# Recurrent-memory attention: last K projection in two banks, second scores earlier, batched Q/K with streaming weights

## The chip, the cores and the metric

The kernel runs on one core of a Trainium2 chip. The metric is the time of one execution on the device, in microseconds (us). A figure for a kernel is the median of several executions.

## The reference

Two residual blocks. The first is attention in segments with a carried memory; the second is a gated mixing block. The change concerns the first alone.

```
for s in range(64):                                  # 2048 rows in segments of 32
    h = concat(mem, xs)                              # 8 memory rows + 32 rows, 512 wide
    q, k, v = h @ Wq, h @ Wk, h @ Wv                 # 32 heads of 128
    p = softmax(mask(q k^T * scale))                 # 40 x 40 for each head
    o = (p v) @ Wo
    mem = o[:8]                                      # memory of the next segment
    outs.append(o[8:])
```

The memory makes the 64 segments strictly sequential: the first rows of the output of segment s are an input of segment s+1. Q, K and V of the 32 rows of a segment itself do not depend on it. Behind the loop stand a layer norm, a GELU projection, a product with a 2048 x 2048 matrix and an output projection.

## The kernel before, in words

`fast_path` records all instructions of five engines in the order of the program; each engine runs its own in that order, and waits are made from tokens that each instruction reads and writes. On every engine the order of the work is therefore the order in which the Python code calls the helpers. One consequence matters here: an instruction that waits holds back all that is recorded behind it on its engine.

The four projection weights stay in SBUF (`arena`, 4 MB each). The 40 rows of a step are split. The 8 memory rows and the first 24 rows of the segment are in `hT` (transposed, 32 columns a step). The last 8 rows of each segment do not depend on the memory and are projected for 16 segments at once: a chunk (`CK` = 16) has 128 such rows, in `hTe`. Their Q and K go to `QTx` (two buffers, one for each of two chunks), their V over DRAM to `Vx`.

**TensorE in four column tiles.** Most matmuls of the loop use the array as four tiles of 128 rows and 32 columns: the 32 columns of `hT` are the weights of each tile, and the projection matrix streams past, 512 columns at a time; tile c computes another quarter of the output. `tile_mm` (L493) emits such a matmul; with `held` it emits one without a weight load (L496 instead of L495), where the tile still holds the same weights.

**One step of the loop** (L945 on), halves b = 0, 1 of 16 heads each:

- `QK` (L501) computes Q or K of one half into a PSUM bank (`QKB`: banks 0, 1, 6, 7), in four groups over the contraction (dc = 0 to 3). dc 0 and 1 need the memory columns from `mem_out(s-1, 0)`, dc 2 and 3 those from `mem_out(s-1, 1)`, which stands between.
- `QK_evac` (L512) brings them from PSUM to `Tst` (ScalarE, L519), pairing heads so that two bf16 values make one 32-bit word, and VectorE transposes the words into `QT` or `KT` (L532). The last K (half 1) is evacuated in two parts, both after its four groups.
- `qx_copy` (L534, GpSimd) puts the 8 batched query rows beside them for the next step.
- `mask_put` (L544) writes the mask into the scores' banks; `S_half` (L546) adds the scores on top: L554 for 32 keys, L560 for the 8 batched keys (from `QTx`).
- Softmax of a half: `sm_exp` (L568, ScalarE), `sm_sums` (two rounds of matmuls with ones, L575 and L496), `sm_ln` (L586), `sm_rcp` (L590, the reciprocal by Exp of the negative logarithm), `sm_norm` (L594 and L598; half 0 on GpSimd, half 1 on VectorE).
- `V_half` (L600) computes V in four groups, `V_evac` (L615, VectorE) copies it.
- `PV_half` (L617): L623 for 32 keys, L629 for the batched 8, with the array as four row tiles.
- `cT_evac` (L642 ScalarE, L644 VectorE), then `WoX_mm` (L707, output product of the batched rows of an earlier block of 128), then `Wo` in two column halves, `part_evac` (L671, L673) and `mem_out` (L680, with its copy L685).

**Filler.** Between the second sums and `PV_half` stands one group per step that nothing in the step waits for: from the list `gx` a batched V group (`vx_group`, L433; steps 1 to 7, 14, 15) or a batched Q/K group (`qkx_group`, L414; steps 8 to 13 and 16 to 47), or, from step 48, a group of the second block (`z2_group`, L775). All go to PSUM bank 3 (`XB`); their evacuation is recorded behind the four `cT_evac`. A second list (`gv`, bank 5) pours single V groups, ahead of the filler or behind `WoX_mm`. In steps with s % 4 = 3, 1, 2 bank 3 is used once more near the step's end.

A batched Q/K group before: four heads, for each four matmuls of the full array (128 x 128 weights taken from `w_q` or `w_k`, 128 streaming columns of `hTe`), copied in one go to `QTx` (`qkx_evac`, L423 on ScalarE ahead of the loop, L425 on VectorE in it). 26 such groups stand ahead of the loop.

Of the kernel before, what the change touches and what calls it, by code (L numbers as in the profile page):

```python
# [169 lines left out]
def fast_path(nc, st, keep, A_x, A_mem0, A_Wq, A_Wk, A_Wv, A_Wo, A_seg_len, B_w_in, B_w_sp, B_b_sp, B_w_out, out):  # L170
# [9 lines left out]
    DC = D // 128  # L180
# [23 lines left out]
    def region(off, n):  # L204
        return arena[:, off:off + n]
# [5 lines left out]
    QTx = [region(4 * WSZ + i * QX, QX).rearrange("p (m s h k) -> p m s h k", m=2, s=CK, h=H) for i in range(2)]  # L211
# [269 lines left out]
    QKB = {(0, 0): 0, (0, 1): 1, (1, 0): 6, (1, 1): 7}  # L481
    SBK = (0, 1)
# [29 lines left out]
    def QK_evac(s, b, mi, parts=1):  # L512
        bank = QKB[(b, mi)]
        tb = mi
        n = 8 // parts
        for k in range(parts):
            tok = [("T", tb, 0), ("T", tb, 1)] if parts == 1 else [("T", tb, k)]
            cs = slice(64 * n * k, 64 * n * (k + 1))
            act(lambda e, cs=cs: e.activation(out=Tst[:, tb, cs].rearrange("p (hp i r) -> p hp i r", i=32, r=2),  # L519
                                              in_=ps[:, bank, cs].rearrange("p (hp r i) -> p hp i r", r=2, i=32), func=ACT.Copy),  # L520
                reads=[PB(bank)], writes=tok)
        for k in range(parts):
            tok = [("T", tb, 0), ("T", tb, 1)] if parts == 1 else [("T", tb, k)]
            src = Tst[:, tb, 64 * n * k:64 * n * (k + 1)].bitcast(U32)
            hs = slice(n * k, n * (k + 1))
            if mi == 0:
                dst = QT[:, b, hs, :, :].rearrange("p hp q r -> p (hp q r)").bitcast(U32).rearrange("p (hp q) -> p hp q", hp=n)[:, :, 8:40]
                wr = [("QT", b)]
            else:
                dst = KT[:, b, hs, :, :].rearrange("p hp q r -> p (hp q r)").bitcast(U32)  # L530
                wr = [("KT", b, 0), ("KT", b, 1)] if parts == 1 else [("KT", b, k)]
            dve(lambda e, dst=dst, src=src: e.transpose(out=dst, in_=src), reads=tok, writes=wr)  # L532

    def qx_copy(s):  # L534
        j = s % CK
        buf = (s // CK) % 2
        dst = QT[:].rearrange("p b hp q r -> p (b hp) q r")[:, :, 0:8, :].rearrange("p hp q r -> p hp r q")
        src = QTx[buf][:, 0, j, :, :].rearrange("p (hp r) q -> p hp r q", r=2)
        pool(lambda e: e.tensor_copy(out=dst, in_=src), reads=[("QTx", buf, 0, i) for i in range(8)],  # L539
             writes=[("QTe", 0), ("QTe", 1)])  # L540
# [5 lines left out]
    def S_half(s, b):  # L546
# [4 lines left out]
        for g in range(4):  # L551
            for c in range(4):
                hp, r = 2 * c + g // 2, g % 2
                pe(lambda e, hp=hp, r=r, c=c, g=g: e.matmul(  # L554
                    ps[32 * c:32 * c + 32, bank, g * 40:(g + 1) * 40], lhsT=KT[:, b, hp, :, r], rhs=QT[:, b, hp, :, r],
                    start=False, stop=(g == 3), skip_group_check=True, tile_position=(0, 32 * c)),
                    reads=rd, writes=[PB(bank)])
# [339 lines left out]

    def vx_group(ck, n):
# [12 lines left out]
    for ck, i0 in ((1, 10), (2, 0), (3, 0)):  # L911
# [3 lines left out]
        for i in range(i0, 16):  # L915
            qkx_group(ck, i)
# [28 lines left out]
    for s in range(NSEG):  # L945
# [1162 lines left out]
```

## Time and profile before

| | us |
|---|---|
| median of 3 runs | 855.01 (853.56 to 855.67) |
| the profiled execution: its own time | 853.86 |
| its span in the profile | 851.7 |
| busy: TensorE matmul | 837.0 |
| busy: VectorE | 538.8 |
| busy: ScalarE | 427.1 |
| busy: GpSimd | 159.8 |

The granted TensorE clock is full speed throughout. Row forms in the timeline: start, duration, engine, line, operation, output tile <- input tiles, shape, count of merged instructions, and in brackets the idle time of the engine before them. "128*32" in front of a matmul's shape gives rows and columns of the array that it uses: 128*128 is the full array, 128*32 one of four column tiles, 32*128 one of four row tiles. The duration of a matmul runs from its start to its last result, longer than the distance to the next one.

### The profile page before, as it was taken

What the parts mean: (1) busy time and instruction counts of PE and PEld (TensorE: products, weight loads), DVE (VectorE), ACT (ScalarE), POOL (GpSimd) and SP (SyncE); (2) the same over time, 40 slices, a digit from 0 to 9 for tenths busy, and PEclk for the clock granted to TensorE, in tenths of its full rate; (3) what the DMA queues carried; (4) which work ended last, traced back from release to release, by engine and by line L of the source; (5) the groups of instructions that cost most, each with busy time, mean ns of one, the idle gap of its engine ahead of it and who ended that gap; (6) DMA issues with size and microseconds to landing.
All of it is one profiled execution on the core that took longest, in us unless ns stands there. A gap on an engine that the chain in (4) does not pass through costs nothing.

```text
span 851.7 us, 43893 instructions
## 1 busy us (share of the span) xinstructions
PE 837.0 (98%) x20921; PEld 447.0 (52%) x19133; DVE 538.8 (63%) x1256; ACT 427.1 (50%) x1151; POOL 159.8 (19%) x404
## 2 busy tenths in 40 slices
PE   6999999999999999999999999999999999999997
PEld 5754445555555555556555555555554544444443
DVE  3456677676666666676766666767666676553443
ACT  2455565656555655555655555565656566500000
POOL 5111121122121112121212121211112123200000
PEclk9999999999999999999999999999999999999999
DMA  9972322223212122121323222233322369032001
GB/s 319 379 227 59 75 56 57 54 47 82 57 34 75 34 65 62 26 72 47 64 58 85 55 74 51 81 70 85 91 57 80 96 184 366 2 112 105 33 12 40
DMA packets 105614, 77.21 MB, mean 91 GB/s; under 512 B 63304, under 2 KB 90960, under 8 KB 105424
## 3 DMA queue, kind: packets, MB, share of 16 engines
q1 hardware_dynamic: 105424, 74.35, 30.3%
q8 instruction: 159, 2.61, 1.3%
q14 instruction: 31, 0.25, 0.1%
HBM read 42.38 MB, written 21.59 MB: 75 GB/s over the span
## 4 chain that ended last, share of the span: by engine, by line
PE 95%; DMA 2%; SPq 1%; issue 0%; ACT 0%; DVE 0%; POOL 0%; POOLq 0%
PE f_ps L495 46%; PE f_ps L1183 11%; PE f_ps L496 8%; PE f_ps L414 6%; PE f_ps L707 4%; PE f_ps L1300 3%; PE f_ps L623 3%; PE f_ps L1176 2%; PE f_ps L433 2%; PE f_ps L775 2%; PE f_ps L554 1%; PE f_ps L575 1%; DMA f_arena<-in_A_Wk_dram 1%; PE f_ps L629 1%; PE f_ps L439 1%; PE f_ps L680 1%
## 5 line engine op out<-in xcount | busy, mean ns | idle before, releaser
L495 PE MATMUL f_ps<-f_arena,f_hT 128*32 128x512 bf16 x5120 | 359.5, 380 | 0.3
L495 PEld LDWEIGHTS f_ps<-f_arena,f_hT 128*32 128x32 bf16 x5120 | 117.0, 95 | 153.7 <-issue 63.0
L519 ACT ACTIVATE f_Tst<-f_ps 128x512 bf16<-128x512 f32 (+1 forms) x320 | 150.0, 510 | 77.5 <-PE f_ps L495 77.4
L495 PE MATMUL f_ps<-f_arena,f_cT 128*32 128x256 bf16 x3844 | 127.9, 272 | 0.7 <-ACT f_cT L642 0.5
L495 PEld LDWEIGHTS f_ps<-f_arena,f_cT 128*32 128x32 bf16 x3844 | 94.8, 96 | 27.3 <-ACT f_cT L642 18.2
L615 DVE CAST f_V_sb<-f_ps 128x512 bf16<-128x512 f32 x128 | 88.6, 692 | 25.4 <-PE f_ps L495 25.4
L1183 PE MATMUL f_ps<-f_arena 128*128 128x512 bf16 x448 | 100.9, 379 | 0.6 <-DMA f_arena<-wT_d 0.6
L532 DVE STREAM_TRANSPOSE f_QT<-f_Tst 128x256 uint32<-128x256 uint32 x128 | 57.0, 446 | 68.6 <-ACT f_Tst L519 68.5
L496 PE MATMUL f_ps<-f_arena,f_hT 128*32 128x512 bf16 x1024 | 99.8, 379 | 0.0
L539 POOL COPY f_QT<-f_arena 128x256 bf16<-128x256 bf16 x64 | 30.8, 482 | 313.3 <-PE f_ps L560 313.2
L642 ACT ACTIVATE f_cT<-f_ps 128x320 bf16<-128x320 f32 x128 | 49.0, 435 | 49.1 <-PE f_ps L629 49.1
L644 DVE TENSOR_SCALAR f_cT<-f_ps 128x320 bf16<-128x320 f32 x128 | 56.9, 487 | 25.4 <-PE f_ps L629 25.4
L532 DVE STREAM_TRANSPOSE f_KT<-f_Tst 128x128 uint32<-128x128 uint32 (+1 forms) x192 | 64.5, 349 | 12.9 <-ACT f_Tst L519 12.9
L1183 PEld LDWEIGHTS f_ps<-f_arena 128*128 128x128 bf16 x448 | 43.7, 98 | 53.4 <-DVE f_mv L723 1.0
L673 DVE CAST f_part<-f_ps 128x256 bf16<-128x256 f32 x64 | 27.2, 425 | 67.9 <-PE f_ps L495 67.9
L414 PE MATMUL f_ps<-f_hTe,f_arena 128*128 128x128 bf16 x1024 | 66.9, 223 | 2.2 <-DMA f_arena<-in_A_Wq_dram 1.4
L414 PEld LDWEIGHTS f_ps<-f_hTe,f_arena 128*128 128x128 bf16 x1024 | 59.1, 100 | 7.5 <-ACT f_hTe L395 1.6
L586 ACT ACTIVATE f_R_sb<-f_ps 128x160 f32<-128x160 f32 x128 | 39.1, 305 | 35.9 <-PE f_ps L496 32.7
L1189 DVE TENSOR_TENSOR f_arena<-f_ps,f_arena 128x512 f32<-128x512 f32 x28 | 19.3, 690 | 52.9 <-PE f_ps L1183 52.9
L685 ACT ACTIVATE f_hT<-f_ps 128x16 bf16<-128x16 f32 x126 | 23.3, 185 | 53.4 <-PE f_ps L680 53.0
L671 ACT ACTIVATE f_part<-f_ps 128x256 bf16<-128x256 f32 x64 | 24.6, 385 | 48.4 <-PE f_ps L495 48.4
L544 DVE CAST f_ps<-f_mask 128x224 f32<-128x224 bf16 x128 | 47.1, 368 | 0.0
(118 smaller groups left out, 1094.1 us busy)
## 6 DMA issues: line engine op xcount, KB each, us to landing
wT_d<-f_wst SPq DMA_DIRECT2D x32, 256.0 KB, 2.5
f_arena<-wT_d SPq DMA_DIRECT2D x32, 256.0 KB, 4.8
f_arena<-in_A_Wq_dram SPq DMA_DIRECT2D x4, 1024.0 KB, 8.7
f_arena<-in_A_Wk_dram SPq DMA_DIRECT2D x4, 1024.0 KB, 14.3
f_arena<-in_A_Wv_dram SPq DMA_DIRECT2D x4, 1024.0 KB, 14.5
f_arena<-in_A_Wo_dram SPq DMA_DIRECT2D x8, 512.0 KB, 9.5
f_Vx<-vext_d SPq DMA_DIRECT2D x63, 64.0 KB, 2.9
vext_d<-f_Vs SPq DMA_DIRECT2D x24, 128.0 KB, 2.0
```

The lines of the kernel that those rows point to most:

```text
L414: pe(lambda e, h=h, dc=dc, hh=hh: e.matmul(ps[:, bank, hh * 128:(hh + 1) * 128], lhsT=ws[:, dc, h * DH:(h + 1) * DH], rhs=hTe[:, ck % 3, d ...
L495: return e.matmul(out, lhsT=lhsT, rhs=rhs, start=start, stop=stop, skip_group_check=True, tile_position=(0, 32 * c))
L496: return e.add_instruction(mybir.InstMatmult(name=nc.get_next_instruction_name(), ins=[e.lower_ap(rhs), e.lower_ap(lhsT)], outs=[e.lower_a ...
L519: act(lambda e, cs=cs: e.activation(out=Tst[:, tb, cs].rearrange("p (hp i r) -> p hp i r", i=32, r=2), in_=ps[:, bank, cs].rearrange("p (h ...
L532: dve(lambda e, dst=dst, src=src: e.transpose(out=dst, in_=src), reads=tok, writes=wr)
L544: dve(lambda e: e.tensor_copy(out=ps[:, bank, 0:224], in_=mask[:, :]), reads=["mask"], writes=[PB(bank)])
L586: act(lambda e: e.activation(out=R_sb[:, b, :], in_=ps[:, bank, 224:384], func=ACT.Ln, scale=LNS), reads=[PB(bank)], writes=[("R", b)])
L615: dve(lambda e: e.tensor_copy(out=V_sb[:, b, :], in_=ps[:, bank, :]), reads=[PB(bank)], writes=[("V", b)])
L642: act(lambda e: e.activation(out=dst, in_=src, func=ACT.Copy, scale=UNSC), reads=[PB(PVB[c])], writes=[("cT", c)])
L644: dve(lambda e: e.tensor_scalar(out=dst, in0=src, scalar1=UNSC, scalar2=None, op0=ALU.mult), reads=[PB(PVB[c])], writes=[("cT", c)])
L707: pe(lambda e, h=h, g=g, i=8 * qr + bg: e.matmul(ps[32 * g:32 * g + 32, WXB, :], lhsT=cTx[:, rb % 2, i, :], rhs=w_o[:, h, :], start=(i < 4 ...
L1183: pe(lambda e: e.matmul(ps[:, bank, 0:TB], lhsT=z2[:, sc, fb * 128:(fb + 1) * 128], rhs=wTb[tb % 2][:, :, sc, :], start=(n == 0), stop=(n ...
```

## The change

1. **Last K in two banks.** K of half 1 is computed by `K1` as two halves of 8 heads, 256 columns each, in banks 3 and 7. The groups of the two alternate so that one ends two groups ahead of the other; `K1_copy` and `K1_transpose` bring each on alone.
2. **Order and held weights in the first half of a step.** Q's dc 0, K's dc 0 with the same weights, the second half of `mem_out`, K's dc 1, Q's dc 1 with the same weights.
3. **Second scores moved forward.** `S_half(s, 1)` stands behind three of the four V groups of half 0 rather than all four, and `sm_ln(0)` behind `sm_exp(1)` rather than ahead of it. The second sums stand ahead of V's last group of half 1 rather than behind it.
4. **Batched Q/K groups.** `qkr_group` takes the 32 rows of four segments as weights of the four column tiles and streams 16 heads of `w_q` or `w_k` past them, 512 columns a matmul, like the projections of a step. ScalarE pairs the heads into `Tst` (`pair_copy`), VectorE transposes into `QTx`. 36 of the 38 groups in the loop have the new form; the first two keep the old one, as do the 26 ahead of it.
5. **Layout.** Pairs are made of heads that are four apart, `QTx` holds them interleaved, and `qx_copy` moves 32-bit words.

```diff
-    QTx = [region(4 * WSZ + i * QX, QX).rearrange("p (m s h k) -> p m s h k", m=2, s=CK, h=H) for i in range(2)]
+    QTx = [region(4 * WSZ + i * QX, QX).rearrange("p (m s C g k r) -> p m s C g k r", m=2, s=CK, C=H // 8, g=4, r=2) for i in range(2)]
+    QTxU = [region(4 * WSZ + i * QX, QX).bitcast(U32).rearrange("p (m s hp k) -> p m s hp k", m=2, s=CK, hp=H // 2) for i in range(2)]
...
+    KB = (3, 7)
...
+    def K1(s, k, dc, first, last, held):
+        bank = KB[k]
+        sl = slot(s)
+        for c in range(4):
+            rhs = w_k[:, dc, :].rearrange("p (h c i) -> p c h i", c=4, i=32)[:, c, 16 + 8 * k:24 + 8 * k, :]
+            pe(lambda e, c=c, rhs=rhs: tile_mm(e, ps[32 * c:32 * c + 32, bank, 0:256], hT[:, sl, dc, :], rhs, first, last, c, held),
+               ...)
+
+    def K1_copy(k):
+        act(lambda e: e.activation(out=Tst[:, 1, 256 * k:256 * k + 256].rearrange("p (gi r) -> p gi r", r=2),
+                                   in_=ps[:, KB[k], 0:256].rearrange("p (r gi) -> p gi r", r=2), func=ACT.Copy),
+            reads=[PB(KB[k])], writes=[("T", 1, k)])
+
+    def K1_transpose(k):
+        src = Tst[:, 1, 256 * k:256 * k + 256].bitcast(U32)
+        dst = KT[:, 1, 4 * k:4 * k + 4, :, :].rearrange("p hp q r -> p (hp q r)").bitcast(U32)
+        dve(lambda e: e.transpose(out=dst, in_=src), reads=[("T", 1, k)], writes=[("KT", 1, k)])
+
+    def pair_copy(bank, tb):
+        act(lambda e: e.activation(out=Tst[:, tb, :].rearrange("p (C gi r) -> p C gi r", C=2, r=2),
+                                   in_=ps[:, bank, :].rearrange("p (C r gi) -> p C gi r", C=2, r=2), func=ACT.Copy),
+            reads=[PB(bank)], writes=[("T", tb, 0), ("T", tb, 1)])
...
+    def qkr_group(ck, mi, b, r):
+        ws = (w_q, w_k)[mi]
+
+        def f():
+            for dc in range(DC):
+                for c in range(4):
+                    rhs = ws[:, dc, :].rearrange("p (h c i) -> p c h i", c=4, i=32)[:, c, 16 * b:16 * b + 16, :]
+                    pe(lambda e, dc=dc, c=c, rhs=rhs: tile_mm(e, ps[32 * c:32 * c + 32, XB, :], hTe[:, ck % 3, dc, 32 * r:32 * r + 32], rhs,
+                                                              dc == 0, dc == DC - 1, c),
+                       ...)
+
+            def ev():
+                pair_copy(XB, 0)
+                dst = QTxU[ck % 2][:, mi, 4 * r:4 * r + 4, 8 * b:8 * b + 8, :].rearrange("p s hp k -> p hp s k")
+                dve(lambda e: e.transpose(out=dst, in_=Tst[:, 0, :].bitcast(U32)), ...)
+            return ev
...
-        QK(s, 0, 0, (0, 1), 0, 3)
+        QK(s, 0, 0, (0,), 0, 3)
+        QK(s, 0, 1, (0,), 0, 2, 0)
         if s > 0:
             mem_out(s - 1, 1)
-        QK(s, 0, 1, (1, 0), 1, 2, None if s else 1)
-        QK(s, 0, 0, (2, 3), 0, 3)
+        QK(s, 0, 1, (1,), 0, 2)
+        QK(s, 0, 0, (1, 2, 3), 0, 3, 1)
...
-        for mi in range(2):
-            QK(s, 1, mi, ((2, 0, 1, 3), (3, 0, 1, 2))[mi], (2, 3)[mi], (3, 2)[mi], (2, 3)[mi])
-            QK_evac(s, 1, mi, 1 + mi)
+        QK(s, 1, 0, (2, 0, 1, 3), 2, 3, 2)
+        QK_evac(s, 1, 0)
+        K1(s, 0, 3, True, False, True)
+        K1(s, 1, 3, True, False, True)
+        K1(s, 0, 0, False, False, False)
+        K1(s, 1, 0, False, False, True)
+        K1(s, 0, 1, False, False, False)
+        K1(s, 0, 2, False, True, False)
+        K1_copy(0)
+        K1(s, 1, 2, False, False, True)
+        K1(s, 1, 1, False, True, False)
+        K1_copy(1)
+        for k in range(2):
+            K1_transpose(k)
         S_half(s, 0)
         sm_exp(0)
-        V_half(s, 0, (0,))
-        if s > 0:
+        if s == 0:
+            V_half(s, 0)
+            V_evac(0, "dve")
+            sm_sums(0)
+            S_half(s, 1)
+        else:
+            V_half(s, 0, (0,))
             V_half(s, 1, (0,), 0)
-        V_half(s, 0, (1, 2, 3))
-        V_evac(0, "dve")
-        sm_sums(0)
-        sm_ln(0)
-        S_half(s, 1)
+            V_half(s, 0, (1, 2))
+            sm_sums(0)
+            S_half(s, 1)
+            V_half(s, 0, (3,))
+            V_evac(0, "dve")
         lastop["s"] = sops[s] = em.by_eng["pe"][-1]
         sm_exp(1)
+        sm_ln(0)
         sm_rcp(0)
         if s == 0:
             for n in range(2, 4):
                 start_v(n)
-        V_half(s, 1, (1, 2, 3) if s > 0 else range(DC))
+            V_half(s, 1)
+            sm_sums(1)
+        else:
+            V_half(s, 1, (1, 2))
+            sm_sums(1)
+            V_half(s, 1, (3,))
         lastop["v"] = em.by_eng["pe"][-1]
-        sm_sums(1)
         sm_ln(1)
         sm_rcp(1)
```

More of the change, by code (lines that the diff above doesn't have):

```diff
@@ L510, in QK @@
                    reads=[("hTx", (s // 4) % 3), ("hTm", s, dc // 2), ("W", mi, 2 * b), ("W", mi, 2 * b + 1)], writes=[PB(bank)])
[L512 to L532, printed above, removed]
@@ new lines, in QK_evac @@
+    def QK_evac(s, b, mi):
+        pair_copy(QKB[(b, mi)], mi)
+        if mi == 0:
+            dst = QT[:, b, :, :, :].rearrange("p hp q r -> p (hp q r)").bitcast(U32).rearrange("p (hp q) -> p hp q", hp=8)[:, :, 8:40]
+            wr = [("QT", b)]
+        else:
+            dst = KT[:, b, :, :, :].rearrange("p hp q r -> p (hp q r)").bitcast(U32)
+            wr = [("KT", b, 0), ("KT", b, 1)]
+        dve(lambda e: e.transpose(out=dst, in_=Tst[:, mi, :].bitcast(U32)), reads=[("T", mi, 0), ("T", mi, 1)], writes=wr)
@@ L536, in qx_copy @@
         buf = (s // CK) % 2
-        dst = QT[:].rearrange("p b hp q r -> p (b hp) q r")[:, :, 0:8, :].rearrange("p hp q r -> p hp r q")
-        src = QTx[buf][:, 0, j, :, :].rearrange("p (hp r) q -> p hp r q", r=2)
+        dst = QT[:].rearrange("p b hp q r -> p (b hp q r)").bitcast(U32).rearrange("p (hp q) -> p hp q", q=40)[:, :, 0:8]
+        src = QTxU[buf][:, 0, j, :, :]
         pool(lambda e: e.tensor_copy(out=dst, in_=src), reads=[("QTx", buf, 0, i) for i in range(8)],
@@ L552, in S_half @@
             for c in range(4):
-                hp, r = 2 * c + g // 2, g % 2
+                hp, r = 4 * (c // 2) + g, c % 2
                 pe(lambda e, hp=hp, r=r, c=c, g=g: e.matmul(
@@ L896, in qkx_group @@
         gx.append(f)
+    def qkr_group(ck, mi, b, r):
[6 more added lines that the diff above has]
+                                                              dc == 0, dc == DC - 1, c),
+                       reads=[("hTe", ck % 3), ("W", mi, 2 * b), ("W", mi, 2 * b + 1)], writes=[PB(XB)])
+            def ev():
+                pair_copy(XB, 0)
+                dst = QTxU[ck % 2][:, mi, 4 * r:4 * r + 4, 8 * b:8 * b + 8, :].rearrange("p s hp k -> p hp s k")
+                dve(lambda e: e.transpose(out=dst, in_=Tst[:, 0, :].bitcast(U32)), reads=[("T", 0, 0), ("T", 0, 1)],
+                    writes=[("QTx", ck % 2, mi, 4 * b + r)])
+            return ev
+        f.full = True
+        gx.append(f)
     def vx_group(ck, n):
@@ L914, in fast_path @@
             vx_group(2, 1)
-        for i in range(i0, 16):
-            qkx_group(ck, i)
+        if i0:
+            qkx_group(ck, 10)
+            qkx_group(ck, 11)
+        for mi, b in ((0, 0), (0, 1), (1, 0), (1, 1))[3 if i0 else 0:]:
+            for r in range(4):
+                qkr_group(ck, mi, b, r)
     for ck, n0 in ((2, 2), (3, 0)):
```

13 lines of the change are left out of this document (8 added, 5 removed).

## The prediction

> **What bounds the kernel now.** I read the page first, then the waits of TensorE, then the timeline of single steps of the loop, engine by engine.
>
> ```profile
> PE 95%; DMA 2%; SPq 1%; issue 0%; ACT 0%; DVE 0%; POOL 0%; POOLq 0%
> ...
> L495 PEld LDWEIGHTS f_ps<-f_arena,f_hT 128*32 128x32 bf16 x5120 | 117.0, 95 | 153.7 <-issue 63.0
> ...
> L414 PE MATMUL f_ps<-f_hTe,f_arena 128*128 128x128 bf16 x1024 | 66.9, 223 | 2.2 <-DMA f_arena<-in_A_Wq_dram 1.4
> ```
>
> TensorE sets the time: 95% of the chain that ended last. L414 is the batched Q/K matmul: 64 groups of 16, of which 26 stand ahead of the loop and 38 in it. Since matmuls overlap, their durations hide small waits; I take start-to-start distances from the timeline. Here is TensorE in one step with a batched Q/K group (starts in us, duration, engine, line, count):
>
> ```profile
> 300.44 0.27 PE L554 MATMUL f_ps<-f_QT,f_KT 128*32 128x40 bf16 x16
> ...
> 300.57 0.39 PE L495 MATMUL f_ps<-f_arena,f_hT 128*32 128x512 bf16 x4
> 300.79 0.39 PE L496 MATMUL f_ps<-f_arena,f_hT 128*32 128x512 bf16 x4
> 301.00 0.82 PE L495 MATMUL f_ps<-f_arena,f_hT 128*32 128x512 bf16 x12
> 301.65 0.24 PE L575 MATMUL f_ps<-f_E_sb,f_ones 128*32 128x160 bf16 x4
> ...
> 301.75 0.27 PE L554 MATMUL f_ps<-f_QT,f_KT 128*32 128x40 bf16 x16
> ...
> 301.88 0.83 PE L495 MATMUL f_ps<-f_arena,f_hT 128*32 128x512 bf16 x12
> 302.56 0.25 PE L575 MATMUL f_ps<-f_E_sb,f_ones 128*32 128x160 bf16 x4
> ...
> 302.78 1.07 PE L414 MATMUL f_ps<-f_hTe,f_arena 128*128 128x128 bf16 x16
> 303.78 0.27 PE L623 MATMUL f_ps<-f_E_sb,f_V_sb 32*128 32x40 bf16 x16
> ...
> 303.99 0.28 PE L623 MATMUL f_ps<-f_E_sb,f_V_sb 32*128 32x40 bf16 x16
> ...
> 304.26 0.61 PE L707 MATMUL f_ps<-f_arena,f_cTx 128*32 128x512 bf16 x8
> ...
> 304.92 1.05 PE L495 MATMUL f_ps<-f_arena,f_cT 128*32 128x256 bf16 x32
> 305.79 0.28 PE L496 MATMUL f_ps<-f_arena,f_cT 128*32 128x256 bf16 x4
> ```
>
> I count from the first score matmul of the first half, 300.44 = 0 (S0). Four 512-column matmuls in four column tiles take 0.215 (300.57 to 301.00 is two such groups). So five V groups bring the first sums at 1.21, the second scores (S1) come at 1.31, three more V groups end at 302.53, and the second sums start at 302.56: 0.03 to 0.04 lost. The batched group (L414), then the first PV half at 3.34, the second at 3.55, and the deferred output product (WoX, L707) at 3.82. I sum to WoX, since the work behind it depends on it alone.
>
> The other engines in the same stretch, first ScalarE, then VectorE, then GpSimd:
>
> ```profile
> 300.66 0.66 ACT L519 ACTIVATE f_Tst<-f_ps 128x256 bf16<-128x256 f32 x2 [0.27 <-PE f_ps L495]
> 301.21 0.36 ACT L568 ACTIVATE f_E_sb<-f_ps 128x224 bf16<-128x224 f32 x1
> 301.96 0.31 ACT L586 ACTIVATE f_R_sb<-f_ps 128x160 f32<-128x160 f32 x1 [0.39 <-PE f_ps L496]
> 302.16 0.35 ACT L568 ACTIVATE f_E_sb<-f_ps 128x224 bf16<-128x224 f32 x1
> 302.41 0.33 ACT L590 ACTIVATE f_R_sb<-f_R_sb 128x160 f32<-128x160 f32 x1
> 302.88 0.30 ACT L586 ACTIVATE f_R_sb<-f_ps 128x160 f32<-128x160 f32 x1
> 303.22 0.34 ACT L590 ACTIVATE f_R_sb<-f_R_sb 128x160 f32<-128x160 f32 x1
> ```
>
> ```profile
> 301.08 0.59 DVE L532 STREAM_TRANSPOSE f_KT<-f_Tst 128x128 uint32<-128x128 uint32 x2 [0.20 <-ACT f_Tst L519]
> ...
> 302.75 0.69 DVE L615 CAST f_V_sb<-f_ps 128x512 bf16<-128x512 f32 x1 [0.18 <-PE f_ps L495]
> 303.59 0.34 DVE L594 TENSOR_TENSOR f_E_sb<-f_R_sb,f_E_sb 128x160 bf16<-128x160 f32 x1
> 303.86 0.21 DVE L598 TENSOR_TENSOR f_E_sb<-f_R_sb,f_E_sb 128x64 bf16<-128x64 f32 x1
> ```
>
> ```profile
> 302.88 0.49 POOL L594 TENSOR_TENSOR f_E_sb<-f_R_sb,f_E_sb 128x160 bf16<-128x160 f32 x1 [0.21 <-ACT f_R_sb L590]
> 303.45 0.31 POOL L598 TENSOR_TENSOR f_E_sb<-f_R_sb,f_E_sb 128x64 bf16<-128x64 f32 x1
> ```
>
> The second PV half starts at 303.99, which is 0.06 after VectorE's normalisation ends (303.59 + 0.34 = 303.93). So in such a step TensorE already waits for the softmax there: sums, Ln, Exp, normalise. That is the key to the forecast.
>
> **The change part by part.**
>
> *Batched group.* Sixteen full-array matmuls become four groups of four tiles, 4 x 0.215 = 0.86. Now, second sums to PV is 303.78 - 302.56 = 1.22. A step with the batched V group, whose matmuls already have the new form, shows the other price:
>
> ```profile
> 191.25 0.25 PE L575 MATMUL f_ps<-f_E_sb,f_ones 128*32 128x160 bf16 x4
> ...
> 192.54 0.27 PE L623 MATMUL f_ps<-f_E_sb,f_V_sb 32*128 32x40 bf16 x16
> 192.67 0.21 PE L629 MATMUL f_ps<-f_E_sb,f_Vx 32*128 32x64 bf16 x4
> ...
> 192.95 0.62 PE L707 MATMUL f_ps<-f_arena,f_cTx 128*32 128x512 bf16 x8
> ```
>
> 1.29 there, with five groups of 0.215 in it; four would be 1.08. The group is thus 0.14 cheaper on TensorE: one of two switches of the array's shape goes. 36 steps have it. Whether the 0.14 reaches the end is decided by PV's waits, below.
>
> *Its evacuation* was one VectorE copy; now it is a ScalarE copy of 128x512 and a VectorE transpose, queued behind the context copies. On ScalarE the tightest place is a step with s % 4 = 3, where the WoX copy (L712) follows:
>
> ```profile
> 244.29 0.60 ACT L712 ACTIVATE f_partx<-f_ps 128x512 bf16<-128x512 f32 x1
> 245.31 0.39 ACT L671 ACTIVATE f_part<-f_ps 128x256 bf16<-128x256 f32 x1 [0.42 <-PE f_ps L495]
> ```
>
> The new copy takes the place at 244.29, L712 moves 0.50 back (0.60, less the 0.1 by which such copies overlap, as the 0.66 for two of 0.38 shows) and ends its turn at 245.29; L671, which the next step's memory rows wait for, is due at 245.31. I take nothing. The other end, without overlap, is 0.3 in 9 steps, 2.8 us. In the other steps an idle stretch of ScalarE covers it. VectorE loses a copy of 128x512 (0.69 as in L615) and gains a transpose (two half ones take 0.59): nothing. The 8-row query copy on GpSimd moves half as many elements; it is not waited for.
>
> *Last K in two banks.* Eight groups of 256 columns for four of 512. L495 with 256 columns goes 304.92 to 305.79 for eight groups, 0.87, against 4 x 0.215 = 0.86: +0.01 a step, 63 steps, **+0.6 us**. In return the first ScalarE copy no longer waits for all of K. Now the two copies start at 0.22 and the exp at 0.77; then the first copy starts at 0.00, the second at 0.28 (ScalarE's pace), the exp at 0.55. Transposes: the first from 0.42, the second behind the second copy, 0.66 + 0.03, to 1.01, not 1.23. The K weights can be used 0.06 later (the PV distance above): 1.07.
>
> *S1 moved forward.* Four V groups instead of five before the first sums: 0.99, and S1 at 1.09. Exp 0 ends at 0.91, so 0.97 for the sums. Both are met with 0.02, about the slack of today (301.57 to 301.65, and 301.67 to 301.75, are 0.08 with the 0.06 in them). I take no wait. Fewer loaded and more held weights in the first half of a step cost and bring nothing: a held group (300.79) takes the same 0.215 as a loaded one.
>
> *The softmax behind it.* Exp 1 started 0.41 after S1, held some 0.05 by the Ln ahead of it; now the exp is first: 1.09 + 0.36 = 1.45 to 1.80. The second sums, after V's last group of half 0 and two of half 1, arrive at 1.87: their 0.04 stall goes. But the first Ln is now behind exp 1: 1.70 to 2.01 (one pace of 0.25 as 302.16 to 302.41), its reciprocal exp 2.04 to 2.37. Today that one ends at 2.30. So half 0 has its reciprocals 0.07 *later*, although everything ahead of it is earlier. GpSimd starts 0.14 behind (302.74 to 302.88): 2.51, the second multiply 0.57 on, 3.08 to 3.39. From a step near the end, without filling work, I read how soon TensorE follows GpSimd:
>
> ```profile
> 679.72 0.31 POOL L598 TENSOR_TENSOR f_E_sb<-f_R_sb,f_E_sb 128x64 bf16<-128x64 f32 x1
> ```
>
> ```profile
> 680.08 0.21 PE L629 MATMUL f_ps<-f_E_sb,f_Vx 32*128 32x64 bf16 x4
> ```
>
> 0.05. So the extra-column matmuls of PV half 0 can start at 3.44, and WoX 0.28 later (192.67 to 192.95): **3.72**. Half 1: Ln at about 2.26 (ScalarE is busy until then), reciprocal 2.60 to 2.94; V's evacuation (L615) starts 0.44 after its last group, now at 1.97, so 2.41 to 3.10; normalise 3.03 to 3.10, the second part 0.27 on, plus 0.21: 3.51 to 3.58; WoX follows that by 0.19 (304.07 to 304.26): 3.70 to 3.77. TensorE alone would have PV at 3.15 and WoX near 3.56. So the two softmax chains set it: 3.72 against 3.82, **0.10 a step**, and most of the cheaper group is waited away.
>
> The steps of the last quarter (z2 filler) end in the same chain today, as sums to WoX shows, 1.70 in both:
>
> ```profile
> 567.62 0.25 PE L575 MATMUL f_ps<-f_E_sb,f_ones 128*32 128x160 bf16 x4
> ...
> 569.32 0.62 PE L707 MATMUL f_ps<-f_arena,f_cTx 128*32 128x512 bf16 x8
> ```
>
> So they gain 0.10 too.
>
> **Sum.** 38 steps with a Q/K group and 16 z2 steps: 54 x 0.10 = 5.4. The 9 V steps have one group more ahead of PV and gain only the sums' stall, 9 x 0.04 = 0.4. K in two banks: -0.6. Together **-5.2 us**. The profiled execution took 853.86 (span 851.7), which would become 848.7; the median of the three runs is 855.01, so I name **849.8**.
>
> **Rivals.**
> - *Deeper gain.* GpSimd answers within 0.08 (the distance between its own two, 303.37 to 303.45) now that its query copy ends early, and VectorE starts to normalise at 2.97, right behind the reciprocal: WoX at 3.63, 0.19 a step, 54 x 0.19 - 0.2 = 10 us, **845**. For it: these are lower ends of rows. Against: GpSimd's 0.14 is what this pair shows, and V's evacuation ends at 3.10.
> - *Weights on the path.* If loads of column tiles did not hide, the 13 loaded groups of a step, now 12, would give 117.0 / 1280 = 0.09 (the page's row of loads, 5120 of them): 63 x 0.09 = 5.8 more, **844**. Against it: 300.57, 300.79 and 301.00 are a loaded, a held and a loaded group, equally spaced within 0.01.
> - *No change.* S1 or the sums miss their 0.02 by 0.05 to 0.09 a step, or the ScalarE queue costs its 2.8: **852.4 to 857**.
> - *Slower.* S1 now waits for the last K transpose. If the two transposes don't overlap with the copies as counted but come a whole one (0.31) later, S1 stands at 1.40, and exp, Ln, GpSimd and PV shift with it: 63 x 0.31 = 19.5, so **869**. It decides from 0.08 a step, and 0.13 makes it slower. For it: 0.02 of slack by rows of two decimals. Against: in the same queue today nothing waits.
> - *It doesn't do what it says*: the cheaper group is there but PV waits; that is the forecast itself.
>
> [...]
>
> **How the numbers follow.** Forecast 848 to 852: 0.57. Deeper gain: 0.20. Weights: 0.01. No change: 0.13. Slower: 0.09. A difference of 0.3%, 2.6 us, is about what a measurement here can tell from none. Faster is 0.57 + 0.20 + 0.01 = 0.78. The range 844.5 to 854 holds the forecast, the deeper gain and the lower part of no change, 0.82.
>
> **What would show it.** L414 falls from 1024 to 448 matmuls. Second sums follow the V group ahead without a gap. PV half 0 stops before its L629 for GpSimd by about 0.15 where a Q/K group stands. S1 at 1.09 behind S0. Wrong if S1 stands later than 1.15, if L671 is late where s % 4 = 3, or if WoX comes before 3.65.

## The result, and the profile after

The changed kernel takes 857.4 us (median of 16 executions, 855.75 to 859.3), the kernel before 854.52 (16 executions, 851.92 to 857.1): a ratio of 1.0033, 95% interval 1.0023 to 1.0043. It is 2.9 us slower, where 5.2 us less had been forecast. The profiled execution of after took 858.33 us, with a span of 856.2.

The first place to look is the chain that ended last. This is its line of shares by engine, on the page of after:

```profile
PE 85%; POOL 6%; ACT 4%; issue 2%; DMA 1%; DVE 0%; SPq 0%; POOLq 0%
```

Before, TensorE had 95% of it and GpSimd 0%. Now GpSimd and ScalarE hold 10% of the chain: part of it has moved from TensorE's own work to the softmax that TensorE waits for. The view of the waits of TensorE's weight loads (PEld; what was waited for, us in total, times, longest) is the next place to look. After:

```profile
PEld f_ps L497 <- issue: 71.0, 197, 0.5
...
PEld f_ps L636 <- POOL f_E_sb L607: 25.2, 61, 0.5
...
PEld f_ps L642 <- POOL f_E_sb L611: 9.1, 39, 0.3
```

And the two rows of before that answer to them:

```profile
PEld f_ps L623 <- POOL f_E_sb L594: 5.9, 16, 0.4
...
PEld f_ps L623 <- POOL f_E_sb L598: 3.8, 9, 0.4
```

PV half 0 is L636 and, for the extra columns, L642. By the view, the loads of L636 wait for GpSimd's first multiply (L607) in 61 steps, those of L642 for the second (L611) in 39. But the filler's matmuls run while these loads wait (in the step below they start at 304.60 and take 1.04, and GpSimd's first multiply ends at 305.42), so the timeline has to tell which of the two waits holds the matmuls up. Here is a step with a batched Q/K group, from the timeline of after, TensorE first:

```profile
302.39 0.27 PE L567 MATMUL f_ps<-f_QT,f_KT 128*32 128x40 bf16 x16
...
303.39 0.24 PE L588 MATMUL f_ps<-f_E_sb,f_ones 128*32 128x160 bf16 x4
...
303.49 0.27 PE L567 MATMUL f_ps<-f_QT,f_KT 128*32 128x40 bf16 x16
...
304.28 0.25 PE L588 MATMUL f_ps<-f_E_sb,f_ones 128*32 128x160 bf16 x4
...
304.60 1.04 PE L497 MATMUL f_ps<-f_arena,f_hTe 128*32 128x512 bf16 x16
305.57 0.27 PE L636 MATMUL f_ps<-f_E_sb,f_V_sb 32*128 32x40 bf16 x16
305.97 0.21 PE L642 MATMUL f_ps<-f_E_sb,f_Vx 32*128 32x64 bf16 x4
306.01 0.26 PE L636 MATMUL f_ps<-f_E_sb,f_V_sb 32*128 32x40 bf16 x16
...
306.24 0.61 PE L720 MATMUL f_ps<-f_arena,f_cTx 128*32 128x512 bf16 x8
```

And the row of before that answers to L642, from the step shown in the prediction, where PV half 0 starts at 303.78:

```profile
303.90 0.21 PE L629 MATMUL f_ps<-f_E_sb,f_Vx 32*128 32x64 bf16 x4
```

PV half 0 starts on time: 0.97 behind the filler (304.60 to 305.57), just as in the first experiment below (302.83 to 303.80), where nothing holds it up and the loads of L636 show a like wait, 24.7 us in 60 steps. So that wait costs nothing. L642 then starts 0.40 behind L636, where before it took 0.12: that is the wait that holds TensorE up.

ScalarE, VectorE and GpSimd of the same step of after:

```profile
303.87 0.36 ACT L581 ACTIVATE f_E_sb<-f_ps 128x224 bf16<-128x224 f32 x1 [0.56 <-PE f_ps L573]
304.12 0.30 ACT L599 ACTIVATE f_R_sb<-f_ps 128x160 f32<-128x160 f32 x1
304.45 0.34 ACT L603 ACTIVATE f_R_sb<-f_R_sb 128x160 f32<-128x160 f32 x1
```

```profile
304.06 1.46 DVE L628 CAST f_V_sb<-f_ps 128x512 bf16<-128x512 f32 x2 [0.66 <-PE f_ps L497]
305.43 0.32 DVE L607 TENSOR_TENSOR f_E_sb<-f_R_sb,f_E_sb 128x160 bf16<-128x160 f32 x1
305.67 0.33 DVE L611 TENSOR_TENSOR f_E_sb<-f_R_sb,f_E_sb 128x64 bf16<-128x64 f32 x1
```

```profile
304.93 0.49 POOL L607 TENSOR_TENSOR f_E_sb<-f_R_sb,f_E_sb 128x160 bf16<-128x160 f32 x1 [0.74 <-ACT f_R_sb L603]
305.50 0.42 POOL L611 TENSOR_TENSOR f_E_sb<-f_R_sb,f_E_sb 128x64 bf16<-128x64 f32 x1
```

The last row is the one to see. GpSimd's second multiply takes 0.42, where it took 0.31 before. It ends at 305.92, and TensorE's L642, which needs it, starts 0.05 later. Counted from the first scores (302.39 = 0), beside what the prediction said:

| | before | predicted | after |
|---|---|---|---|
| first sums | 1.21 | 0.99 | 1.00 |
| second scores (S1) | 1.31 | 1.09 | 1.10 |
| Exp of half 1 | 1.72 | 1.45 | 1.48 |
| Ln of half 0 | 1.52 | 1.70 | 1.73 |
| second sums | 2.12 | 1.87 | 1.89 |
| GpSimd's second multiply | 3.01 to 3.32 | 3.08 to 3.39 | 3.11 to 3.53 |
| VectorE's first multiply | 3.15 | 3.03 | 3.04 |
| PV half 0 | 3.34 | 3.15 by TensorE alone | 3.18 |
| extra-column matmuls of PV half 0 | 3.46 | 3.44 | 3.58 |
| WoX | 3.82 | 3.72 | 3.85 |

A step with a batched V group ends in the same place. TensorE and GpSimd in one of after:

```profile
190.19 0.27 PE L567 MATMUL f_ps<-f_QT,f_KT 128*32 128x40 bf16 x16
...
193.77 0.21 PE L642 MATMUL f_ps<-f_E_sb,f_Vx 32*128 32x64 bf16 x4
...
194.04 0.40 PE L720 MATMUL f_ps<-f_arena,f_cTx 128*32 128x512 bf16 x4
```

```profile
193.29 0.42 POOL L611 TENSOR_TENSOR f_E_sb<-f_R_sb,f_E_sb 128x64 bf16<-128x64 f32 x1
```

Its WoX stands at 194.04 - 190.19 = 3.85 too. In a z2 step of after (first scores at 567.70) L642 follows at 571.27 and WoX at 571.54, 3.57 and 3.84. So every kind of step has the same softmax chain as its bound, and the 0.14 that the new group saves TensorE is waited away.

The regular steps account for about 2 us. By medians over the loop (start of one Exp of half 0 to the next), a V step went from 10.081 to 10.120 (9 steps), a Q/K step from 10.119 to 10.155 (38), a z2 step from 10.096 to 10.123 (15): 0.35 + 1.37 + 0.41 = 2.1 us. The two profiled spans differ by 4.5; the other 2.4 are single stalls inside the loop (1.1) and the part behind it (1.3), which single executions show and which I do not interpret.

### The profile page after: what moved, and what is told of

The parts are those of the page before. It is cut to its first block, busy times and chain, and to the rows that moved or that the text cites. A ratio compares the mean times of both kernels' runs of the same rounds, so it can differ in the third digit from the quotient of the medians.

```text
span 856.2 us, 44699 instructions
## 1 busy us (share of the span) xinstructions
PE 834.0 (97%) x21945; PEld 426.1 (50%) x18881; DVE 533.3 (62%) x1256; ACT 444.3 (52%) x1187; POOL 153.9 (18%) x404
## 4 chain that ended last, share of the span: by engine, by line
PE 85%; POOL 6%; ACT 4%; issue 2%; DMA 1%; DVE 0%; SPq 0%; POOLq 0%
PE f_ps L497 37%; PE f_ps L498 12%; PE f_ps L1243 11%; PE f_ps L720 4%; PE f_ps L1360 3%; PE f_ps L1236 2%; PE f_ps L434 2%; POOL f_E_sb L607 2%; POOL f_E_sb L611 2%; PE f_ps L788 2%; PE f_ps L415 2%; PE f_ps L642 2%; ACT f_E_sb L581 2%; ACT f_R_sb L603 2%; PE f_ps L567 1%
## 5 line engine op out<-in xcount | busy, mean ns | idle before, releaser
L497 PE MATMUL f_ps<-f_arena,f_hT 128*32 128x512 bf16 (+1 forms) x4868 | 356.7, 357 | 0.5 <-issue 0.2
L497 PEld LDWEIGHTS f_ps<-f_arena,f_hT 128*32 128x32 bf16 x4868 | 121.8, 95 | 155.0 <-issue 69.5
L498 PE MATMUL f_ps<-f_arena,f_hT 128*32 128x512 bf16 x2300 | 183.2, 331 | 0.0
L533 ACT ACTIVATE f_Tst<-f_ps 128x512 bf16<-128x512 f32 x228 | 129.5, 597 | 60.9 <-PE f_ps L497 60.9
L552 POOL COPY f_QT<-f_arena 128x128 uint32<-128x128 uint32 x64 | 18.7, 292 | 299.8 <-PE f_ps L573 299.7
L581 ACT ACTIVATE f_E_sb<-f_ps 128x224 bf16<-128x224 f32 x128 | 46.3, 362 | 36.4 <-PE f_ps L573 36.4
L603 ACT ACTIVATE f_R_sb<-f_R_sb 128x160 f32<-128x160 f32 x128 | 43.1, 337 | 4.1
L523 ACT ACTIVATE f_Tst<-f_ps 128x256 bf16<-128x256 f32 x128 | 42.1, 381 | 3.7
L677 POOL COPY f_cTx<-f_cT 128x256 bf16<-128x256 bf16 x64 | 25.4, 396 | 102.1 <-DVE f_cT L657 102.1
L607 POOL TENSOR_TENSOR f_E_sb<-f_R_sb,f_E_sb 128x160 bf16<-128x160 f32 x64 | 31.3, 489 | 54.3 <-ACT f_R_sb L603 53.2
```

Of the source, the lines that this page charges most:

```text
L497: return e.matmul(out, lhsT=lhsT, rhs=rhs, start=start, stop=stop, skip_group_check=True, tile_position=(0, 32 * c))
L498: return e.add_instruction(mybir.InstMatmult(name=nc.get_next_instruction_name(), ins=[e.lower_ap(rhs), e.lower_ap(lhsT)], outs=[e.lower_a ...
L533: act(lambda e: e.activation(out=Tst[:, tb, :].rearrange("p (C gi r) -> p C gi r", C=2, r=2), in_=ps[:, bank, :].rearrange("p (C r gi) -> ...
L581: act(lambda e: e.activation(out=E_sb[:, b, :], in_=ps[:, bank, 0:224], func=ACT.Exp, scale=scale, bias=SHIFT), reads=[PB(bank)], writes=[ ...
L603: act(lambda e: e.activation(out=R_sb[:, b, :], in_=R_sb[:, b, :], func=ACT.Exp, scale=-1.0, bias=RBIAS), reads=[("R", b)], writes=[("R", b)])
L607: on(lambda e: e.tensor_tensor(out=E_sb[:, b, 0:160], in0=R_sb[:, b, :], in1=E_sb[:, b, 0:160], op=ALU.mult), reads=[("R", b), ("E", b)], ...
```

## The experiments

Three theories stood against each other. **A**: the second multiplies collide. GpSimd's chain came later, VectorE's earlier, they now run at the same time and each makes the other longer. **B**: GpSimd's multiply has become longer of its own, by where it stands or by what its data are. **C**: the evacuation of the new groups, by ScalarE and VectorE, costs the time. All kernels below compute the full reference.

### Ln of half 0 ahead of Exp of half 1 again

```diff
-        sm_exp(1)
         sm_ln(0)
+        sm_exp(1)
         sm_rcp(0)
```

> The changed kernel with the Ln of half 0 back ahead of the Exp of half 1 on ScalarE. Theory A (two second multiplies, GpSimd's and VectorE's, run beside each other and each takes 0.11 us longer, which holds the first PV half): GpSimd's chain starts about 0.3 us earlier, so its second multiply goes back from 0.42 to 0.31 us and ends ahead of VectorE's; the extra-column matmuls of PV half 0 no longer wait; WoX stands at about 3.75 us behind the first scores instead of 3.85; the second sums wait 0.04 for the Exp. Time 54 x 0.10 + 9 x 0.03 = 5.7 below the changed kernel, about 851.7 where the kernel before has 854.5. Theory B (GpSimd's second multiply is longer of its own, whatever runs beside it): it stays at 0.42, but its chain is early enough all the same; time like A. Theory C (the evacuation of the new batched groups over ScalarE and VectorE costs the time): within 1 us of the changed kernel, 857.

Measured: 852.81 us (850.69 to 854.33), ratio to before 0.9966, interval 0.9952 to 0.998. The timeline of this kernel, GpSimd, VectorE and TensorE of the same step, with the first scores at 300.59:

```profile
302.82 0.49 POOL L607 TENSOR_TENSOR f_E_sb<-f_R_sb,f_E_sb 128x160 bf16<-128x160 f32 x1 [0.40 <-ACT f_R_sb L603]
303.39 0.31 POOL L611 TENSOR_TENSOR f_E_sb<-f_R_sb,f_E_sb 128x64 bf16<-128x64 f32 x1
```

```profile
303.66 0.32 DVE L607 TENSOR_TENSOR f_E_sb<-f_R_sb,f_E_sb 128x160 bf16<-128x160 f32 x1
303.90 0.22 DVE L611 TENSOR_TENSOR f_E_sb<-f_R_sb,f_E_sb 128x64 bf16<-128x64 f32 x1
```

```profile
300.59 0.27 PE L567 MATMUL f_ps<-f_QT,f_KT 128*32 128x40 bf16 x16
...
302.83 1.04 PE L497 MATMUL f_ps<-f_arena,f_hTe 128*32 128x512 bf16 x16
303.80 0.27 PE L636 MATMUL f_ps<-f_E_sb,f_V_sb 32*128 32x40 bf16 x16
303.92 0.21 PE L642 MATMUL f_ps<-f_E_sb,f_Vx 32*128 32x64 bf16 x4
...
304.04 0.28 PE L636 MATMUL f_ps<-f_E_sb,f_V_sb 32*128 32x40 bf16 x16
...
304.31 0.40 PE L720 MATMUL f_ps<-f_arena,f_cTx 128*32 128x512 bf16 x4
```

GpSimd's second multiply is nearly over (303.70) when VectorE's first starts (303.66); it takes 0.31 again, and VectorE's second 0.22. WoX stands at 3.72. A Q/K step is 10.014 long, 0.105 less than before. PV half 0 does not stop any more: L642 starts 0.12 behind L636. This one line of order is worth 4.6 us by the medians (857.4 to 852.81) and 5.7 by the two ratios to before (1.0033 and 0.9966), where theory A had 5.7, and this kernel is faster than before and after. It does not yet tell A from B, since GpSimd's whole chain has moved as well.

### VectorE's multiplies moved away, GpSimd left where it is

```diff
         V_evac(1, "dve")
+        V_evac(1, "dve")
         sm_norm(1, dve)
```

The copy of V is made twice, so VectorE starts to multiply later; GpSimd's chain keeps its place.

> The changed kernel with VectorE's copy of V, half 1, made twice in a row, so that VectorE's two multiplies come 0.6 us later and GpSimd's second multiply has only a copy out of PSUM beside it. Theory A: GpSimd's second multiply takes 0.31 instead of 0.42, VectorE's second 0.21 instead of 0.33, and the extra-column matmuls of PV half 0 start at 3.47 us behind the first scores instead of 3.58, though the step as a whole is 0.47 longer (time about 887). Theory B: GpSimd's second multiply stays at 0.42, the extra columns at 3.58.

Measured: 889.4 us (one execution). GpSimd, VectorE and TensorE of the step, from its timeline:

```profile
317.64 0.31 POOL L611 TENSOR_TENSOR f_E_sb<-f_R_sb,f_E_sb 128x64 bf16<-128x64 f32 x1
```

```profile
318.30 0.32 DVE L607 TENSOR_TENSOR f_E_sb<-f_R_sb,f_E_sb 128x160 bf16<-128x160 f32 x1
```

```profile
314.53 0.27 PE L567 MATMUL f_ps<-f_QT,f_KT 128*32 128x40 bf16 x16
...
318.00 0.21 PE L642 MATMUL f_ps<-f_E_sb,f_Vx 32*128 32x64 bf16 x4
```

GpSimd's second multiply starts at 317.64 - 314.53 = 3.11, exactly as in after, and takes 0.31, not 0.42. The extra-column matmuls follow at 3.47, where the prediction had 3.44. That settles A against B: what makes the multiply longer is VectorE's multiply beside it; VectorE's copies, which stand beside it here, leave it at 0.31. (The time itself is longer, as expected, because PV half 1 now waits for VectorE, 0.47 in the step shown. So this run shows what the collision does to L642, not to the time.) The durations over all 64 steps, lowest, median and highest in ns, say the same, of before, after and this kernel in turn:

```profile
L598 POOL TENSOR_TENSOR f_E_sb<-f_R_sb,f_E_sb x64: 305/308/338, 42.6 to 689.7; 128x64 bf16<-128x64 f32 x64
```

```profile
L611 POOL TENSOR_TENSOR f_E_sb<-f_R_sb,f_E_sb x64: 304/416/477, 43.0 to 693.2; 128x64 bf16<-128x64 f32 x64
```

```profile
L611 POOL TENSOR_TENSOR f_E_sb<-f_R_sb,f_E_sb x64: 303/304/308, 43.2 to 723.9; 128x64 bf16<-128x64 f32 x64
```

### The batched groups in their old form

```diff
-        if i0:
-            qkx_group(ck, 10)
-            qkx_group(ck, 11)
-        for mi, b in ((0, 0), (0, 1), (1, 0), (1, 1))[3 if i0 else 0:]:
-            for r in range(4):
-                qkr_group(ck, mi, b, r)
+        for i in range(i0, 16):
+            qkx_group(ck, i)
```

> The changed kernel with all batched Q/K groups in the old form (full array, one VectorE copy). Theories A and B: the dearer group, 0.14 a step, fills time in which PV waits anyway; WoX stays at 3.85 behind the first scores and the time within 1.5 us of the changed kernel, 857. Theory C: about 3 us below the changed kernel, like the kernel before, 854.5.

Measured: 856.62 us (856.51 to 858.92), ratio to before 1.0035, interval 1.0019 to 1.005: not to be told from after's 1.0033. A Q/K step is 10.142 long, against 10.155. In the step that starts at 302.43, L642 stands at 3.58 and WoX at 3.84, as in after. C falls: without the new evacuation the loss is the same. The 0.14 that TensorE gains by the new groups is worth nothing here.

### The new groups alone, in the order of before

The edit is the reverse of points 1 to 3 of the change; layout and `qkr_group` stay.

```diff
-        K1(s, 0, 3, True, False, True)
...
+        for mi in range(2):
+            QK(s, 1, mi, ((2, 0, 1, 3), (3, 0, 1, 2))[mi], (2, 3)[mi], (3, 2)[mi], (2, 3)[mi])
...
+        V_half(s, 0, (1, 2, 3))
+        V_evac(0, "dve")
+        sm_sums(0)
+        sm_ln(0)
+        S_half(s, 1)
```

> The loop of the kernel before (order, last K in one bank, Ln first, sums behind V) with the new batched groups and the new layout alone. Theories A and B: the first PV half is asked for 0.14 earlier, but the second half waits for the same softmax chain (3.55 behind the first scores), so WoX stays at 3.82 and the time within 1 us of the kernel before, 854.5. Theory C: 2 us or more above it.

Measured: 854.7 us (852.72 to 856.2), ratio 1.0002, interval 0.9993 to 1.0012. A Q/K step is 10.113 long, before's 10.119. The loss of after thus belongs to points 1 to 3 of the change, the order of the step, and the new groups by themselves do nothing, for the same reason: in before's order too, PV waits for the softmax.

### V of half 1 copied by two engines

In the best version PV half 1 waits for VectorE, whose multiply stands behind its copy of V (303.66 above). Here VectorE copies 256 columns and ScalarE the other 256, on top of the first experiment.

```diff
+        if eng == "both":
+            dve(lambda e: e.tensor_copy(out=V_sb[:, b, 0:256], in_=ps[:, bank, 0:256]), ..., writes=[("V", b)])
+            act(lambda e: e.activation(out=V_sb[:, b, 256:512], in_=ps[:, bank, 256:512], func=ACT.Copy), ..., writes=[("V2", b)])
...
-        V_evac(1, "dve")
+        V_evac(1, "both")
```

> The changed kernel with the Ln of half 0 ahead of the Exp of half 1 (as in the run before), and V's evacuation of half 1 split: 256 columns on VectorE, 256 on ScalarE behind the reciprocal. Theory A (PV waits for the softmax chain; with the early Ln the last wait is VectorE's multiply, held by its own 0.69 us copy of V): the multiply starts right behind the reciprocal, 0.13 earlier; PV half 1 no longer waits (0.08 to 0.10 now); steps with a batched Q/K group take 9.91 instead of 10.01, z2 steps about 9.90, V steps stay at 10.09. Time 5 below the run before, about 847.5. Theory B (TensorE is already the bound there, or ScalarE's new copy delays the context copies): 852 to 853.

Measured: 852.51 us (850.99 to 853.96), ratio 0.998, interval 0.9971 to 0.9989: faster than before, but not beyond the first experiment. The time that theory B named came out, not theory A's. VectorE, ScalarE and TensorE from its timeline, first scores at 300.90:

```profile
303.36 0.42 DVE L626 CAST f_V_sb<-f_ps 128x256 bf16<-128x256 f32 x1
303.83 0.34 DVE L607 TENSOR_TENSOR f_E_sb<-f_R_sb,f_E_sb 128x160 bf16<-128x160 f32 x1
```

```profile
303.82 0.38 ACT L627 ACTIVATE f_V_sb<-f_ps 128x256 bf16<-128x256 f32 x1
```

```profile
304.10 0.27 PE L640 MATMUL f_ps<-f_E_sb,f_V_sb 32*128 32x40 bf16 x16
304.23 0.21 PE L646 MATMUL f_ps<-f_E_sb,f_Vx 32*128 32x64 bf16 x4
304.35 0.28 PE L640 MATMUL f_ps<-f_E_sb,f_V_sb 32*128 32x40 bf16 x16
...
304.59 0.61 PE L724 MATMUL f_ps<-f_arena,f_cTx 128*32 128x512 bf16 x8
```

Half of theory A holds: VectorE's multiply starts at 2.93 instead of 3.07. The two copies of V take turns, as the program's tokens order it for two engines that read one PSUM bank: VectorE's ends at 303.78, ScalarE's starts at 303.82 and ends at 304.20. But PV half 1 (the second L640) does not wait for it. By the medians it starts 0.125 behind L646 in every kind of step, although the last copy has ended 0.15 ahead of it in a Q/K step and 0.37 ahead in a V step. In the first experiment, where PV half 1 waits for nothing either in a V step, that distance is 0.03, as in before's V step (192.67 to 192.70). So the wait is gone, and PV half 1 still starts 0.10 later behind L646 than there: Q/K steps shrink only to 9.994 (from 10.014), z2 steps grow to 10.049 (from 9.994) and V steps to 10.166 (from 10.087). In this kernel PV half 1 has two engines to wait for, VectorE and ScalarE, instead of one; whether that is what costs the 0.10 was not tried.

### The same with the old groups

> The run before (early Ln, split copy of V) with all batched Q/K groups in the old full-array form. Theory A: once PV waits for nothing, the dearer group shows: steps with a batched Q/K group 0.10 to 0.14 longer (10.02 to 10.05), 36 of them, 4 to 5 us above the split copy alone, about 852. Theory B (the group's form never matters): the same time as the split copy alone.

The edit to the groups is that of the third experiment. Measured: 856.06 us (855.07 to 857.89), ratio 1.0023, interval 1.0013 to 1.0033. A Q/K step is 10.135 long, against 9.994 with the new groups: 0.14, what the prediction worked out for the cheaper group. PV half 0 starts at 3.34 (305.28 - 301.94) against 3.20, and the parts of PV follow one another by 0.125 in both kernels. In 36 steps that is 5 us, and 856.06 - 852.51 = 3.6 by the medians, where theory A had 4 to 5. The step itself is longer than its 10.02 to 10.05, since the kernel it builds on had not become as short as expected. So the new groups do gain, once the softmax is early enough for PV not to wait.

### The last K in one bank

```diff
-        K1(s, 0, 3, True, False, True)
...
-        K1(s, 1, 1, False, True, False)
+        QK(s, 1, 1, (3, 0, 1, 2), 3, 2, 3)
...
+        QK_evac(s, 1, 1, 2)
```

> The changed kernel with the last K back in one bank, four groups of 512 columns and both copies behind them; the moved second scores stay. Theory A: the transposes end at 1.23 us behind the first scores instead of 1.01, the second scores start at 1.30 instead of 1.10, and with them Exp, Ln, GpSimd and PV move by 0.20: 63 x 0.20 = 12.6 above the changed kernel, about 869. Theory B (K's two banks are not needed for the move): within 2 us of the changed kernel, 857.

Measured: 868.62 us (one execution). Its first and second scores and VectorE's transposes of K, from the timeline:

```profile
305.73 0.27 PE L575 MATMUL f_ps<-f_QT,f_KT 128*32 128x40 bf16 x16
...
307.02 0.27 PE L575 MATMUL f_ps<-f_QT,f_KT 128*32 128x40 bf16 x16
```

```profile
306.37 0.59 DVE L530 STREAM_TRANSPOSE f_KT<-f_Tst 128x128 uint32<-128x128 uint32 x2 [0.20 <-ACT f_Tst L540]
```

S1 stands at 1.29 instead of 1.10: the two banks buy 0.19 a step, 63 x 0.19 = 12 us, and 868.62 - 857.4 = 11.2 were measured. That part of the change does what it says.

### GpSimd's two multiplies in the other order

GpSimd does the small multiply of half 0 first, then the large one, on top of after. It asks which of the two engines gives way.

```diff
-        sm_norm(0, pool)
+        sm_norm_swapped(0, pool)
```

> The changed kernel with GpSimd's two multiplies of half 0 in the other order: the small one (64 columns) first, where VectorE has no multiply running, then the large one (160), beside both of VectorE's. Theory A1 (only the two small, strided multiplies hold each other up): GpSimd's small one takes 0.31, its large one stays at 0.49, VectorE's small one goes from 0.33 back to 0.22; the time stays within 2 us of the changed kernel, since PV half 0 now starts with the large part (3.47) and its extra columns follow at 3.59. Theory A2 (any multiply of GpSimd is held up beside any of VectorE's): the large one takes 0.6 or more and the time is some 7 us above, 864.

Measured: 860.92 us (one execution). GpSimd and VectorE from its timeline, first scores at 303.49:

```profile
306.03 0.30 POOL L616 TENSOR_TENSOR f_E_sb<-f_R_sb,f_E_sb 128x64 bf16<-128x64 f32 x1 [0.74 <-ACT f_R_sb L603]
306.42 0.49 POOL L617 TENSOR_TENSOR f_E_sb<-f_R_sb,f_E_sb 128x160 bf16<-128x160 f32 x1
```

```profile
306.54 0.55 DVE L607 TENSOR_TENSOR f_E_sb<-f_R_sb,f_E_sb 128x160 bf16<-128x160 f32 x1
307.00 0.21 DVE L611 TENSOR_TENSOR f_E_sb<-f_R_sb,f_E_sb 128x64 bf16<-128x64 f32 x1
```

Neither theory came out whole. GpSimd's two durations, VectorE's small one and the times of PV (3.47 and 3.58) are those of A1. But VectorE's large multiply, which starts 0.12 behind GpSimd's, takes 0.55 instead of 0.32, which neither theory had. The time is 3.5 us above after because PV half 0 now needs the large multiply, the later of the two, before it can start: WoX stands at 3.92.

In after, VectorE started first by 0.07 (305.43 and 305.50), and GpSimd was the one to become longer. So in both kernels the engine that starts second pays, GpSimd in the one and VectorE in the other, and the first keeps its time (0.32 and 0.49). How much it pays can be read too: VectorE starts 0.37 ahead of GpSimd's end (306.54 to 306.91) and pays 0.23. In after GpSimd starts 0.25 ahead of VectorE's end (305.50 to 305.75) and pays 0.11. It is the time that the first one still needs, less 0.14, in both.

## Why the prediction was wrong

- **The failed step** is this one: "GpSimd starts 0.14 behind (302.74 to 302.88): 2.51, the second multiply 0.57 on, 3.08 to 3.39." The start was right to 0.03 (3.11). The duration was taken from before, 0.31, and was 0.42. In before, VectorE's first multiply began 0.14 into GpSimd's second (303.59 and 303.45), and GpSimd's stayed at 0.31. In after it begins 0.07 ahead of it. With VectorE's multiplies moved away, GpSimd's takes 0.31 again from the same start, and L642 stands at 3.47. The text had both times, 3.08 for the one and 3.03 for the other, a few sentences apart, and did not ask how long two multiplies take that run at the same time.
- **How that makes the sum.** L642 at 3.58 instead of 3.44, WoX at 3.85 instead of 3.72: 0.13 in 54 steps is 7.0 us. The V steps, counted at -0.04, came out 0.04 longer because the same chain reaches them: 9 x 0.08 = 0.7. From -5.2 that leads to +2.5. The regular steps measured make +2.1; the rest of the 2.9 lies in the stalls and behind the loop, so that 2.5 comes near 2.9 is in part luck. Without the collision an estimate of WoX is 3.47 + 0.27 = 3.74 (L642 as in the second experiment, WoX behind it as in after), which is the forecast to 0.02. No run shows that kernel.
- **Ln behind Exp.** The prediction saw that the first Ln comes later "although everything ahead of it is earlier", and priced the delay at 0.07. The delay was right. Its consequence was not: 0.10 later for GpSimd's second multiply and 0.11 earlier for VectorE's first is what brings the two together.
- **What was right.** First sums, S1, second sums without a gap, and PV's waiting for the two softmax chains, each to 0.03. L415, which was L414, fell to 448 matmuls. TensorE follows GpSimd by 0.05. The ScalarE queue where s % 4 = 3 takes the new copy: L684, the copy that was L671, starts 1.76 behind WoX there as in the other steps, and only takes 0.398 instead of 0.383. The gain of the cheaper group is 0.14 where nothing waits, and is waited away here, as counted; 0.11 of it stands ahead of the group, which before starts 0.14 behind the second round of the sums (302.64 to 302.78), where a V group starts 0.03 behind it (191.33 to 191.36). The two K banks, counted at 0.01 a step, cost that: from WoX to the next first scores a Q/K step takes 6.300 in after and 6.290 in the run with one bank, by the medians. None of the three signs of being wrong came (S1 at 1.10, L684 on time, WoX not before 3.65). What did tell was the stop of PV half 0 ahead of its extra columns: 0.28 (0.40 less 0.12), where about 0.15 had been forecast.
- **The rivals.** The slower one (S1 behind a late K transpose) did not happen; the slower side came by another mechanism, which the list did not hold. "Deeper gain" was wrong in the same step: it set GpSimd's and VectorE's multiplies at their lower ends without looking at them together.
- **What stays open.** With the order of the first experiment the regular steps are 38 x 0.105 + 15 x 0.102 = 5.5 us shorter than before's, yet the ratio 0.9966 is 2.9. In its profiled execution single stalls inside the loop add up to 4.7 us, before's to 2.4. The "issue" row of the loads (time in which they waited for nothing that the profile shows), 71.0 us in after and 63.6 before, does not explain it: it is 70 to 71 in every run with K in two banks, the fastest included, and 62 to 64 in the three kernels with one. What causes these single stalls was not tried. Nor were point 2 of the change and the earlier second sums tried by themselves.

## What to carry to other kernels

Before moving a step, lay the new start and end times of all engines side by side, and look for pairs of operations, here GpSimd's and VectorE's multiplies, that did not run together in the old order: a duration from the old trace was measured beside the neighbours it had there, and GpSimd's 0.31 became 0.42 beside another. Where two chains end close together, it matters less that all of the work is earlier than which chain's tail is delayed: here an Exp put ahead of a Ln cost some 5 us, more than the rest of the change brought. A long wait of a weight load says little until the matmuls behind it are seen to start late: the 25.2 us of L636 cost nothing here. A saving on a busy engine is real only in steps where that engine does not wait (the cheaper group brought 0.14 a step with the split copy and nothing in after's order), so free the wait first and then count it.

## What the runs showed of the hardware

In these kernels, where GpSimd's multiply of `R_sb` and `E_sb` ran beside VectorE's for 0.16 to 0.37 us, the one that started second became longer and the first kept its time. In the four pairings that recur in the loop the second paid what the first still had to run, less 0.13 to 0.14 us:

| second, and kernel | alone | here | time left of the first | longer by |
|---|---|---|---|---|
| VectorE 128x160, before | 0.315 | 0.342 | 0.16 | 0.03 |
| GpSimd 128x64, after | 0.304 | 0.416 | 0.25 | 0.11 |
| VectorE 128x64, after | 0.218 | 0.329 | 0.25 | 0.11 |
| VectorE 128x160, last experiment | 0.315 | 0.548 | 0.37 | 0.23 |

These are medians over the loop; alone is how long they take in the kernel with the copy made twice, where no two multiplies overlap. In the first experiment 0.04 is left (303.66 to 303.70), and VectorE's 128x160 takes 0.315, as alone. From these rows the prediction's own two starts, 3.08 and 3.03, give an estimate of 0.13 for what GpSimd's second multiply pays (VectorE's 0.32 from 3.03 leaves 0.27, and 0.14 comes off). VectorE's copies out of PSUM did not lengthen a multiply of GpSimd: in after, GpSimd's first multiply lies beside the V copy (304.93 to 305.42, the copies until 305.52) and keeps its 0.49, as in all 64 steps:

```profile
L607 POOL TENSOR_TENSOR f_E_sb<-f_R_sb,f_E_sb x64: 486/489/492, 42.4 to 692.6; 128x160 bf16<-128x160 f32 x64
```
